# Batch 0's attention in f32 straight from the inputs, its probabilities turned by TensorE, its chunks in the order 1, 0, 2

## The chip, the cores and the metric

The kernel runs on one core of one Trainium2 chip. Its metric is the device time in microseconds (us), here the median of three executions. A measurement of it tells a difference of about 1% from none. PE is TensorE, PEld its weight loads, DVE VectorE, ACT ScalarE, POOL GpSimd, SP SyncE; POOL and SP here mostly copy and issue transfers, and ACT's queue issues the loads of the inputs.

## The reference, cut to what matters

Block-sparse attention over four batches, eight heads, 768 positions of 64 numbers, and a bilinear FFN (512 to 1536 to 512) on its result. A query block of 32 rows sees its own block and its neighbours, the first and the last block, and three drawn blocks; the first and the last query block see everything.

```python
scores = scale * np.matmul(q, k.transpose(0, 1, 3, 2))
mask = np.abs(blk_i - blk_j) <= window
mask = mask | (blk_i == 0) | (blk_j == 0) | (blk_i == n_blocks - 1) | (blk_j == n_blocks - 1)
for qb in range(n_blocks):
    for kb in sampled_blocks[qb]:
        mask[qb * block:(qb + 1) * block, kb * block:(kb + 1) * block] = True
scores = np.where(mask, scores, -1000000000.0)
scores = scores - np.max(scores, axis=-1, keepdims=True)
attn = np.exp(scores)
attn = attn / (np.sum(attn, axis=-1, keepdims=True) + 1e-09)
x = np.matmul(attn, v)          # then (3072, 512)
a = x @ w_a
b = x @ w_b
return (a * b @ w_out).astype(np.float32)
```

q, k, v and the drawn blocks are f32 and int64, the three weights float64.

## The kernel before

**Units and chunks.** A unit is one query block of one batch with all eight heads (24 units a batch; units 0 and 23 are dense, the others sparse with 256 keys). Eight units are a chunk of 256 tokens, three chunks a batch, twelve in all. Every operand of a matmul that isn't f32r is split into a high and a low f16 part, and a product is three products (high by high, high by low, low by high).

**Preparation.** `keys` loads one pair of heads of K, finds its largest value (ACT, L477), a scale of a power of two (`set_scale`: POOL, then three DVE steps), and makes both parts (ACT L482, DVE L483); SP turns them by a DMA transpose into `keysT`. `values` does the same for V (L522, L523) and stores the parts in DRAM (`vd`). `queries` does it for a chunk (L637 to L644) and copies the parts to the other half of the partitions over SP. `weights` turns float64 bits into f32 (three DVE steps, L699, L702, L705) and splits: the columns of w_a and w_b into f16 parts (`wab`, ACT L719 and L726, DVE L727), w_out into two f32r parts (`woh`, `wol`, L732 and L733). The staging space of the weights is that of K and V of later batches and of `keysT[1]`, so batch 1 starts its loads behind the last weight (`w_freed`).

**Attention.** For a sparse unit POOL copies the keys that it sees into `KG`, SP fetches its values into `VG`; `attend` sends a mask product (L853) and 16 score products (L752) to PE, the largest score (DVE L868), the exponentials with sums (ACT L878), the reciprocal, and `in_parts` splits the probabilities (ACT L770 or DVE L773, then DVE L777) into `hl`. SP turns `hl` by a DMA transpose into `pt`; 24 value products (L796) follow. A dense unit goes the same way in four pieces (`attend_quad`, `all_values`). Each pair of units gives `xT` (ACT L1040, DVE L1043).

**FFN.** `first_products` sends 24 products (L1078) a column f of 128, twelve columns a chunk, into one of two PSUM banks `ab`; `inner` multiplies both halves, `split` makes the f32r parts, `second_products` sends six products (L1166 to L1168) a column into `o`. The second chunk in order is parked: its products are stored in DRAM and fetched back later (`parked_g`).

**What sets the order.** The kernel is written as flows (generators) that yield steps; a planner gives each engine's steps a place by the costs, ranks and events written beside them, and the program is that list. Each engine then runs its list in order, waiting where a semaphore says so. `units` and its numbers `order` set which unit comes when; rings (`take`) bound how many buffers are in use.

Of the kernel before, what the change touches and what calls it, by code (L numbers as in the profile page):

```python
# [18 lines left out]
NB = 24  # L19
# [223 lines left out]
def kernel(  # L243
# [9 lines left out]
    c_blocks: bass.AP,  # L253
    out: bass.AP,
# [51 lines left out]


# [18 lines left out]

    k_ready = [Event(NG) for _ in range(B)]
# [5 lines left out]
    q_ready = [Event(3) for _ in range(NC)]  # L333
    tables = Event()
    mask_ready = Event()
    units = [(b, i) for b in range(B) for i in range(NB)]
# [42 lines left out]
    def make_tables():  # L379
# [3 lines left out]
        row = work.tile([P, DM], F32, tag="st", name="mrow", bufs=ST_BUFS)  # L383
        held2 = yield from take("st", ST_BUFS)
# [9 lines left out]
        def load():  # L394
# [7 lines left out]
            nc.scalar.dma_start(cb, c_blocks)  # L402

        yield [Way("ACT", 300, load, 250)]
# [43 lines left out]
    def raw_tile(b, g, n):  # L448

        if b == 0:  # L450
            late = wab[:, NF // 2 :].rearrange("p f i a c x -> p (f i a c x)").bitcast(F32)
            late = late.rearrange("p (g x) -> p g x", x=2 * NT * D)
            return late[:, n * NG + g], parked
# [8 lines left out]
    parked = Event(2 * NG)  # L462

    def keys(b, g):
        yield from gate(order[b, 0] - GATE_KV)
# [4 lines left out]
        elif b > 0:  # L470
# [27 lines left out]
    def values(b, g):  # L498
# [17 lines left out]
        if g == NG - 1:  # L516
            plan.start(values_scale(b), order[b, 0] - LEAD_V)
        yield v_scale[b]
# [33 lines left out]

    def gather_keys(n):
# [8 lines left out]
        to = KG[n % KG_BUFS].bitcast(I32)  # L562
        of = keysT[b % 2].bitcast(I32)
        w = BLK // 2
        first = i <= KG_BUFS

        def copies():
# [4 lines left out]
            for r, at in enumerate(dynamic("POOL", offs_k, i)):  # L572
# [7 lines left out]

    def gather_values(n):
# [3 lines left out]
        yield v_stored[b]  # L585
# [3 lines left out]
        to = VG[n % VG_BUFS]  # L589
        first = i <= VG_BUFS  # L590

        def copies():
            if i in (0, NB - 1):
                hq, x1 = divmod(x, 2)
                nc.sync.dma_start(
                    to.rearrange("p a x -> p (a x)")[:, : 3 * ROW // HQ].rearrange(
                        "p (t x) -> p t x", t=3
                    ),
                    vd[b][x1 * HALF : (x1 + 1) * HALF, hq * ROW // HQ : (hq + 1) * ROW // HQ]
# [3 lines left out]
            nc.sync.dma_start(to[0 : 3 * BLK, 0, :], vd[b][(i - 1) * BLK : (i + 2) * BLK, :])  # L603
            if first:
                nc.sync.dma_start(to[3 * BLK : P, 0, :], vd[b][0:BLK, :])
                nc.sync.dma_start(to[0:BLK, 1, :], vd[b][(NB - 1) * BLK :, :])
            for r, at in enumerate(dynamic("SP", offs, i)):
                nc.sync.dma_start(  # L608
                    to[(1 + r) * BLK : (2 + r) * BLK, 1, :], vd[b][bass.ds(at, BLK), :]
                )  # L610

        dense = i in (0, NB - 1)
# [660 lines left out]
```

## Time and profile before

| | |
|---|---|
| median of three executions | 959.56 us (955.2 to 962.41) |
| span of the profiled execution, first to last instruction | 943.8 us (23,877 instructions) |
| its own time | not listed apart from the three; span and median differ by 15.8 us |
| PE busy | 784.2 us, 83% |
| DVE busy | 580.2 us, 61% |
| ACT busy | 459.2 us, 49% |
| POOL busy | 173.6 us, 18% |
| DMA | 145.24 MB, 154 GB/s on average |

Busy time is the union of an engine's instructions; matmuls are pipelined, so a group's mean duration is longer than the distance from one start to the next, and prices of matmuls are read from starts. Idle time of an engine that nobody waits for costs nothing.

### The profile page before, as it was taken

Reading aid. Unit: us, or ns where it says so; the run is one execution under the profiler, and the core shown is the slowest. Engines: PE = TensorE matmul, PEld = TensorE weight load, DVE = VectorE, ACT = ScalarE, POOL = GpSimd, SP = SyncE. Lnnn points to the kernel's source line nnn. Section 1 sums busy time; section 2 is a strip of 40 time slices with the busy share of each in tenths; the row PEclk is TensorE's granted clock in tenths of the full one; section 3 lists DMA queues with packets and bytes.
Section 4 is the critical chain, followed back from the end, with each engine's and each line's share of the span. In section 5 each row is a group of like instructions: output and inputs, shape, how many; then the busy total and the mean of one; then the engine's idle time right before and its main releaser. Section 6 shows DMA issues by size and latency. Waiting matters only on the chain.

```text
span 943.8 us, 23877 instructions
## 1 busy us (share of the span) xinstructions
PE 784.2 (83%) x9024; PEld 628.9 (67%) x9024; DVE 580.2 (61%) x1593; ACT 459.2 (49%) x1097; POOL 173.6 (18%) x416
## 2 busy tenths in 40 slices
PE   0133388868978889989989989999999999999998
PEld 0022267646756767778767877777777778888886
DVE  3797899985646766755667766555764735432222
ACT  4665455685525655744455566334554424332222
POOL 0344320221003433100233221000441300000000
PEclk9999589988998999999999999999999999999999
DMA  9999998489878779894775995644675605432000
GB/s 260 252 237 181 217 246 239 130 218 167 202 183 175 157 160 233 193 193 110 161 166 130 249 164 141 155 99 124 163 152 122 139 1 138 111 79 63 22 2 23
DMA packets 212030, 145.24 MB, mean 154 GB/s; under 512 B 152777, under 2 KB 180426, under 8 KB 211146
## 3 DMA queue, kind: packets, MB, share of 16 engines
q1 hardware_dynamic: 201088, 105.95, 52.0%
q10 hardware_dynamic: 10826, 37.76, 13.9%
q8 instruction: 71, 1.16, 0.5%
q14 instruction: 45, 0.37, 0.1%
HBM read 87.56 MB, written 14.16 MB: 108 GB/s over the span
## 4 chain that ended last, share of the span: by engine, by line
PE 42%; DMA 24%; DVE 18%; ACT 7%; SPq 5%; issue 4%; ACTq 0%; POOL 0%; DVEq 0%
PE ab L1078 23%; DMA pt<-hl 12%; PE o L1166 4%; PE av L796 4%; PE o L1168 4%; PE o L1167 4%; DVE hl L777 3%; PE s L752 2%; DMA VG<-vd 2%; DVE hl L773 2%; DMA q<-in_q_dram 2%; ACT sm L878 2%; DVE low L868 2%; SPq L608 1%; DVE xT L1043 1%
## 5 line engine op out<-in xcount | busy, mean ns | idle before, releaser
L1078 PE MATMUL ab<-xT,wab 128*128 128x256 f16 x3456 | 410.8, 277 | 12.8 <-ACT xT L1040 5.0
L1078 PEld LDWEIGHTS <-wab 128*128 128x128 f16 x3456 | 332.4, 99 | 85.1 <-issue 38.0
L1113 DVE TENSOR_TENSOR a<-a,ab 128x256 f32<-128x256 f32 x144 | 60.2, 418 | 122.5 <-ACT a L1110 121.1
L878 ACT ACTIVATE sm<-s,low,cq 128x256 f32<-128x256 f32 x176 | 98.1, 560 | 76.4 <-DVE hl L777 44.1
L1166 PE MATMUL o<-woh,gh 128*128 128x512 f32 x288 | 126.9, 441 | 8.1 <-ACT gh L1135 7.9
L1110 ACT ACTIVATE a<-ab,f 128x256 f32<-128x256 f32 x144 | 67.7, 470 | 134.1 <-PE ab L1078 126.7
L796 PE MATMUL av<-pt,VG 128*128 128x64 f16 x2688 | 107.4, 198 | 27.3 <-DMA VG<-vd 17.7
L796 PEld LDWEIGHTS <-VG 128*128 128x128 f16 x2688 | 98.3, 101 | 46.9 <-issue 36.4
L777 DVE SCALAR_TENSOR_TENSOR hl<-sm,den,hl 128x256 f16<-128x256 f32 (+1 forms) x208 | 106.1, 516 | 16.4 <-ACT hl L770 14.3
L1168 PE MATMUL o<-woh,gl 128*128 128x512 f32 x288 | 115.3, 400 | 1.0 <-DVE gl L1138 1.0
L1167 PE MATMUL o<-wol,gh 128*128 128x512 f32 x288 | 113.8, 395 | 0.0
L568 POOL COPY KG<-keysT 128x384 int32<-128x384 int32 x88 | 52.5, 596 | 318.6 <-PE s L752 285.2
L573 POOL COPY KG<-keysT 128x128 int32 x264 | 95.3, 398 | 42.4 <-POOL KG L568 30.7
L773 DVE TENSOR_SCALAR hl<-sm,den 128x256 f16<-128x256 f32 (+1 forms) x140 | 53.3, 382 | 60.8 <-DMA pt<-hl 60.5
L1135 ACT CAST gh<-a 128x256 fp32r<-128x256 f32 x132 | 53.2, 403 | 68.9 <-DVE a L1113 68.0
L752 PEld LDWEIGHTS <-QT 128*32 128x32 f16 x1664 | 45.3, 104 | 50.8 <-issue 46.5
L853 PE MATMUL s<-mrows,ident 128*32 128x192 bf16 (+1 forms) x352 | 26.2, 286 | 63.2 <-ACT sm L878 41.3
L1138 DVE TENSOR_TENSOR gl<-a,gh 128x256 fp32r<-128x256 f32 x132 | 58.2, 441 | 32.6 <-ACT gh L1135 31.1
L1166 PEld LDWEIGHTS o<-woh,gh 128*128 128x128 f32 x288 | 54.6, 190 | 28.0 <-ACT gh L1135 11.5
L1043 DVE SCALAR_TENSOR_TENSOR xT<-av,xT 64x256 f16<-64x256 f32 x96 | 40.4, 421 | 52.2 <-ACT xT L1040 51.1
L1168 PEld LDWEIGHTS o<-woh,gl 128*128 128x128 f32 x288 | 54.7, 190 | 16.2 <-DVE gl L1138 3.8
L853 PEld LDWEIGHTS <-ident 128*32 128x32 bf16 x352 | 11.9, 94 | 76.7 <-issue 67.8
(93 smaller groups left out, 797.9 us busy)
## 6 DMA issues: line engine op xcount, KB each, us to landing
VG<-vd SPq DMA_DIRECT2D x280, 64.0 KB, 2.5
VG<-vd SPq DMA_DIRECT2D x88, 192.0 KB, 3.5
VG<-vd SPq DMA_DIRECT2D x32, 384.0 KB, 3.6
q<-in_q_dram ACTq DMA_DIRECT2D x12, 512.0 KB, 5.7
QT<-QT SPq DMA_DIRECT2D x24, 256.0 KB, 4.2
vd<-vs SPq DMA_DIRECT2D x16, 384.0 KB, 3.9
out_dram<-ou SPq DMA_DIRECT2D x24, 256.0 KB, 3.3
stage<-in_k_dram ACTq DMA_DIRECT2D x12, 384.0 KB, 5.7
```

Source lines behind the costliest of these rows:

```text
L573: nc.gpsimd.tensor_copy(to[:, :, (5 + r) * w : (6 + r) * w], of[:, :, bass.ds(at, w)])
L752: mm(to[h * BLK : (h + 1) * BLK], q_block(cc, i, 4 * hq + h, a), rhs(4 * hq + h), start=(first and a == 0), stop=(a == 1), skip_group_chec ...
L773: Way("DVE", 227 + n * 0.49, lambda: nc.vector.tensor_scalar(hi, sm, over, None, ALU.mult), 0, X_HIGH),
L777: t = yield dve(221 + n * 1.03, lambda: nc.vector.scalar_tensor_tensor(lo, sm, over, hi, ALU.mult, ALU.subtract))
L796: mm(av[:, g, i % 2, :], w, pt[:, y, cols], start=(i % 2 == 0 and g == 0 and first and n + m == 0), stop=(last and n == len(terms) - 1 and ...
L878: t = yield act(750, lambda hq=hq: nc.scalar.activation(sm[:, hq], ps[:, hq], AF.Exp, bias=low[:, at, hq, 0:1], scale=cq[:, cc, hq : hq + ...
L1078: mm(ab[:, i, :], wab[:, f, i, part, kt, :], xc[:, kt, a, :], start=(i == 0 and kt == 0 and part + a == 0), stop=(kt == KT - 1 and a == 1) ...
L1110: yield act(470, lambda: nc.scalar.activation(a_sb, ab[:, 0, :], AF.Copy, scale=fb[:, f : f + 1]))
L1113: t = yield dve(420, lambda: nc.vector.tensor_mul(a_sb, a_sb, ab[:, 1, :]))
L1166: mm(po, gh[:, js], woh[:, f, :], start=(f == 0), stop=False)
L1167: mm(po, gh[:, js], wol[:, f, :], start=False, stop=False)
L1168: mm(po, gl[:, js], woh[:, f, :], start=False, stop=(f == NF - 1))
```

## The change

For batch 0 alone, nothing is split. K is laid out on the host as it is used (head pair on the partitions, keys along) and loaded into `keysT[0]` as f32; V is laid out by position and gathered from the input itself, so `vd` of batch 0 isn't written; only V's largest value is still taken, for the scale of x, which moves into `output_half`. Queries are loaded into a tile of which one half of the partitions is zero (even heads have the upper half zero, odd heads the lower), so that one product over 128 rows takes one head of a pair. Scores are 8 f32 products a sparse unit instead of 16, values 8 instead of 24. The probabilities are normalised in place (`plain_norm`), turned by four f32 transposes on PE into a PSUM bank of the ring `ab` (`plain_turn`, against an identity that is loaded as a new constant), and copied to `pt`. The bank of `ab` is the one that the FFN's products use.

The order of batch 0's chunks is 1, 0, 2 (`seq`): the eight sparse units 8 to 15 come first, then dense unit 0 with 1 to 7. The first chunk in order is not parked, the second is, as before. The queries' rows of all batches are laid out even heads first.

```diff
+    plain_keys = keysT[0].rearrange("p h s -> p (h s)").bitcast(F32).rearrange(
+        "p (g s) -> p g s", g=NG
+    )
+    plain_values = v[0].rearrange("g p x -> (g p x)").rearrange("(s x) -> s x", x=H * D)
...
+    seq = [1, 0, *range(2, NC)]
+    place = {cc: p for p, cc in enumerate(seq)}
...
-    units = [(b, i) for b in range(B) for i in range(NB)]
+    units = [divmod(cc, NCH) for cc in seq]
+    units = [(b, c * PER + x) for b, c in units for x in range(PER)]
...
     def keys(b, g):
+        if b == 0:
+            t = yield load_way(1000, lambda: nc.scalar.dma_start(plain_keys[:, g], k[0, g]))
+            k_ready[0].fire(t)
+            if g + 1 < NG:
+                plan.start(keys(0, g + 1), -LEAD_K)
+            return
...
         v_bound[b].fire(end)
         if g == NG - 1:
             plan.start(values_scale(b), order[b, 0] - LEAD_V)
+        if b == 0:
+            freed.fire(end)
+            return
...
+    def plain_queries(cc, u0):
+        q_used[cc] = yield from take("QT", QT_BUFS)
+        t = work.tile([P, 2, NG, CH], F32, tag="QT", name=f"QZ{cc}", bufs=QT_BUFS)
+        QT[cc] = t
+        parts_of = [slice(0, D), slice(D, P)]
+        def blank():
+            for y in range(2):
+                nc.gpsimd.memset(t[parts_of[1 - y], y], 0.0)
+        end = yield pool(1800, blank)
+        for y in range(2):
+            end = yield load_way(700, lambda y=y: nc.scalar.dma_start(
+                t[parts_of[y], y], q[0, cc, :, y * NG : (y + 1) * NG]
+            ))
+            q_ready[cc].fire(end)
+        next_queries(cc)
...
+    def plain_scores(to, cc, i, hq, rhs, first):
+        r = i % PER * BLK
+        for h in range(4):
+            g, y = divmod(4 * hq + h, 2)
+            mm(
+                to[h * BLK : (h + 1) * BLK], QT[cc][:, y, g, r : r + BLK], rhs(g),
+                start=first, stop=True, skip_group_check=True,
+            )
...
+    def plain_norm(sm, over, n):
+        return [
+            Way("DVE", 150 + n * 0.53, lambda: nc.vector.tensor_scalar(
+                sm, sm, over, None, ALU.mult
+            )),
+            Way("ACT", 290 + n * 0.83, lambda: nc.scalar.activation(
+                sm, sm, AF.Copy, scale=over
+            )),
+        ]
+    def plain_turn(sm, pt, name, freed):
+        cols = pt.shape[1]
+        yield eye_ready
+        read = yield from take("ab", 2)
+        ps = psum.tile([P, cols, P], F32, tag="ab", name=f"tp{name}", bufs=2)
+        def turns_():
+            for x in range(cols):
+                nc.tensor.transpose(ps[:, x], sm[:, x * P : (x + 1) * P], eye[0])
+        t = yield pe(110 * cols, turns_)
+        freed.fire(t)
+        eye_used.fire(t)
+        n = cols * P
+        t = yield [
+            Way("ACT", 220 + n * 0.83, lambda: nc.scalar.copy(pt, ps)),
+            Way("DVE", 160 + n * 1.04, lambda: nc.vector.tensor_copy(pt, ps)),
+        ]
+        read.fire(t)
+        return t
...
+        if b == 0:
+            yield dve(165, lambda: nc.vector.tensor_scalar(dn, dn, EPS, None, ALU.add))
+            yield dve(160, lambda: nc.vector.reciprocal(dn, dn))
...
+            for hq in range(HQ):
+                yield plain_norm(sm[:, hq], den[:, at, hq, 0:1], NK)
...
+            yield from plain_turn(sm.rearrange("p a k -> p (a k)"), pt, f"{n}", freed)
...
-        if cc >= 2:
-            yield ffn_done[cc - 2]
+        p = place[cc]
+        if p >= 2:
+            yield ffn_done[seq[p - 2]]
+        if b == 0:
+            yield v_scale[0]
...
+        s = float(2.0 ** -14)
+        if cc < NCH:
+            s = scale[half * 64 : half * 64 + 64, at_v : at_v + 1]
```

Where the lists of the engines change, at three places (names with a number are buffers). SP's queue near its start, before: `keysT` is K turned, `QT` the queries' second half, `vd` V's parts in DRAM.

```order
L491 DMA_TRANSPOSE keysT_77<-ks_3_144 128x12x128
L668 DMA QT_140<-QT_140 64x2048
L527 DMA vd_79<-vs_2_306 128x6x256
L527 DMA vd_79<-vs_3_307 128x6x256
L527 DMA vd_79<-vs_1_308 128x6x256
L995 DMA_TRANSPOSE pt_00_350<-hl_00_334 128x6x128
L527 DMA vd_79<-vs_0_340 128x6x256
```

SP's queue at its start now: the gathers of the first two units' values, from the input.

```order
L647 DMA VG_85<-in_v_dram 96x512
L649 DMA VG_85<-in_v_dram 32x512
L650 DMA VG_85<-in_v_dram 32x512
L573 TENSOR_LOAD offs
L652 ISA
L652 DMA VG_85<-in_v_dram 32x512
```

Ahead of the first sparse unit's gather (L603) stood 21 transfers of the preparation and of the first dense unit; now none does.

DVE's list up to the last x step of the first chunk (`xT`), before: splitting probabilities (`hl`) and weights (`wol`, `wab`) stand side by side.

```order
L733 TENSOR_TENSOR wol<-w_1007,woh 128x512
L375 RECIPROCAL scale<-rscale 128x2
L702 SCALAR_TENSOR_TENSOR wab<-stage,wab 128x512
L777 SCALAR_TENSOR_TENSOR hl_1281<-sm_1175,den,hl_1281 128x256
L705 SCALAR_TENSOR_TENSOR wab<-stage,wab 128x512
L727 SCALAR_TENSOR_TENSOR wab<-wab,scale 128x512 x2
L699 TENSOR_SCALAR wab<-stage 128x512
L1043 SCALAR_TENSOR_TENSOR xT_87<-av_6_1277,xT_87 64x4x64 x2
```

The same place now (`pt` is the copy of turned probabilities, `tp` the PSUM bank); it is row 133 of the list instead of 248.

```order
L801 TENSOR_TENSOR wol<-w_389,woh 128x512
L386 RECIPROCAL scale<-rscale 128x2
L773 SCALAR_TENSOR_TENSOR wab<-keysT_78,wab 128x512
L770 SCALAR_TENSOR_TENSOR wab<-keysT_78,wab 128x512
L795 SCALAR_TENSOR_TENSOR wab<-wab,scale 128x512
L948 COPY pt_00_785<-tp_00_786 128x384
L795 SCALAR_TENSOR_TENSOR wab<-wab,scale 128x512
L1211 SCALAR_TENSOR_TENSOR xT_87<-av_14_735,scale,xT_87 64x4x64 x2
```

The same x step comes after fewer weight steps, and no split of probabilities stands ahead of it.

PE's list ahead of the first product of the FFN (`ab`), before: the value products of the first chunk's last units end in it.

```order
L853 LDWEIGHTS ident
...
L752 LDWEIGHTS QT_140
...
L796 LDWEIGHTS VG_85
L796 MATMUL av_6_1277<-pt_1173,VG_85 128x64
L1078 LDWEIGHTS wab
L1078 MATMUL ab_0_1431<-xT_87,wab 128x256
```

The same place now (`s_00` to `s_11` are scores of dense unit 0):

```order
L878 MATMUL av_12_611<-pt_638,VG_86 128x64 x8
L878 MATMUL av_14_735<-pt_680,VG_85 128x64 x8
L820 MATMUL s_10_757<-keysT_77,QZ_130 32x384 x4
L940 MATMUL tp_00_786<-eye,sm_00_753 128x128 x3
L878 MATMUL av_14_735<-pt_716,VG_86 128x64 x8
L820 MATMUL s_11_763<-keysT_77,QZ_130 32x384 x4
L940 MATMUL tp_01_818<-eye,sm_01_756 128x128 x3
L1246 LDWEIGHTS wab
L1246 MATMUL ab_0_826<-xT_87,wab 128x256
```

The first product stands behind the first half of the dense unit, its scores and its turns.

## Rows read from the trace of the kernel before

**Rows 1.** The page, slices: TensorE, busy tenths in 40 equal slices.

```profile
PE   0133388868978889989989989999999999999998
```

**Rows 2.** Windows of the span: busy time of each engine, granted clock, DMA share.

```profile
core 0: us, PE busy (x) PEld busy (x) DVE busy (x) ACT busy (x) POOL busy (x), PEclk, DMA share, GB/s
0.00:125.40 125.40, 32.65 (x532) 23.65 (x533) 94.17 (x255) 71.47 (x152) 40.30 (x82) 0.89 0.99 231
125.40:189.00 63.60, 56.08 (x572) 45.17 (x571) 60.36 (x161) 37.73 (x89) 11.34 (x22) 0.92 0.72 199
189.00:272.00 83.00, 66.65 (x678) 51.58 (x676) 51.78 (x145) 47.59 (x109) 11.02 (x31) 0.92 0.85 191
272.00:431.00 159.00, 138.76 (x1815) 109.89 (x1813) 107.62 (x307) 89.54 (x217) 40.81 (x100) 0.96 0.86 184
431.00:944.00 513.00, 490.02 (x5436) 398.57 (x5432) 266.27 (x729) 212.89 (x533) 70.09 (x181) 1.00 0.49 114
```

**Rows 3.** Timeline of PE around the first product: start, us, engine, line, what, idle before.

```profile
125.44 0.58 PE L1078 MATMUL ab<-xT,wab 128*128 128x256 f16 x2 [3.65 <-ACT xT L1040]
...
132.68 0.86 PE L796 MATMUL av<-pt,VG 128*128 128x64 f16 x24
...
133.47 0.27 PE L853 MATMUL s<-mrows,ident 128*32 128x192 bf16 x4
...
133.56 0.61 PE L752 MATMUL s<-KG,QT 128*32 128x256 f16 x16
...
134.10 2.79 PE L1078 MATMUL ab<-xT,wab 128*128 128x256 f16 x24
...
136.74 0.86 PE L796 MATMUL av<-pt,VG 128*128 128x64 f16 x24
...
137.75 0.39 PE L1167 MATMUL o<-wol,gh 128*128 128x512 f32 x1
...
137.98 0.40 PE L1168 MATMUL o<-woh,gl 128*128 128x512 f32 x1
```

**Rows 4.** Timeline of DVE: the last weight's step L733, same columns.

```profile
188.67 0.69 DVE L733 TENSOR_TENSOR wol<-w,woh 128x512 fp32r<-128x512 f32 x1
```

**Rows 5.** Groups by line, DVE: count, busy us, mean ns, idle before.

```profile
L777 DVE SCALAR_TENSOR_TENSOR hl<-sm,den,hl 128x256 f16<-128x256 f32 (+1 forms) x208 | 106.1, 516 | 16.4 <-ACT hl L770 14.3
...
L773 DVE TENSOR_SCALAR hl<-sm,den 128x256 f16<-128x256 f32 (+1 forms) x140 | 53.3, 382 | 60.8 <-DMA pt<-hl 60.5
...
L644 DVE SCALAR_TENSOR_TENSOR QT<-q,scale,QT 64x2048 f16<-64x2048 f32 x12 | 28.2, 2349 | 8.7 <-ACT QT L642 8.7
...
L727 DVE SCALAR_TENSOR_TENSOR wab<-wab,scale 128x512 f16<-128x512 f32 x16 | 12.1, 768 | 0.0
...
L483 DVE SCALAR_TENSOR_TENSOR ks<-stage,scale,ks 128x768 f16<-128x768 f32 x12 | 11.9, 1014 | 1.1 <-ACT ks L482 1.0
...
L1182 DVE COPY ou<-o 128x512 f32<-128x512 f32 x13 | 8.8, 687 | 1.8 <-PE o L1168 1.8
...
L733 DVE TENSOR_TENSOR wol<-w,woh 128x512 fp32r<-128x512 f32 x12 | 8.4, 701 | 0.0
...
L705 DVE SCALAR_TENSOR_TENSOR w<-keysT,w 128x512 int32<-128x512 int32 x10 | 7.0, 704 | 0.0
...
L702 DVE SCALAR_TENSOR_TENSOR w<-stage,w 128x512 int32<-128x512 int32 x10 | 6.8, 682 | 0.0
...
L699 DVE TENSOR_SCALAR w<-keysT 128x512 int32<-128x512 int32 x10 | 4.2, 428 | 0.0
```

**Rows 6.** Groups by line, PE and its weight loads (PEld), same columns.

```profile
L1078 PE MATMUL ab<-xT,wab 128*128 128x256 f16 x3456 | 410.8, 277 | 12.8 <-ACT xT L1040 5.0 <-ACT wab L726 4.1 <-DVE power L369 2.1
...
L796 PE MATMUL av<-pt,VG 128*128 128x64 f16 x2688 | 107.4, 198 | 27.3 <-DMA VG<-vd 17.7 <-DMA pt<-hl 6.5 <-DVE xT L1043 2.8
...
L796 PEld LDWEIGHTS <-VG 128*128 128x128 f16 x2688 | 98.3, 101 | 46.9 <-issue 36.4 <-DMA VG<-vd 8.4 <-DMA keysT<-in_moe_w_out_dram 0.4
...
L1168 PEld LDWEIGHTS o<-woh,gl 128*128 128x128 f32 x288 | 54.7, 190 | 16.2 <-DVE gl L1138 3.8
```

More of the change, by code (lines that the diff above doesn't have):

```diff
@@ L383, in make_tables @@
         row = work.tile([P, DM], F32, tag="st", name="mrow", bufs=ST_BUFS)
+        rings.setdefault("hl", Ring(HL_BUFS)).freed.append(eye_used)
+        whole = work.tile([P, 2 * HQ * NK // 2], F32, tag="hl", name="eye", bufs=HL_BUFS)
+        eye[0] = whole[:, :P]
         held2 = yield from take("st", ST_BUFS)
@@ L452, in raw_tile @@
             late = late.rearrange("p (g x) -> p g x", x=2 * NT * D)
[L453 removed]
+            return late[:, g], parked
         yield w_freed
@@ L879, in attend @@
                 sm[:, hq], ps[:, hq], AF.Exp, bias=low[:, at, hq, 0:1],
-                scale=cq[:, cc, hq : hq + 1], accum_out=den[:, at, hq, 0:1],
+                scale=factor_of(b, cc, hq), accum_out=den[:, at, hq, 0:1],
             ))
         read.fire(t)
+        if b == 0:
+            yield dve(165, lambda: nc.vector.tensor_scalar(dn, dn, EPS, None, ALU.add))
+            yield dve(160, lambda: nc.vector.reciprocal(dn, dn))
+            mine = yield from turn("hl", b, i)
+            mine.fire(0)
+            for hq in range(HQ):
+                yield plain_norm(sm[:, hq], den[:, at, hq, 0:1], NK)
+            mine = yield from turn("pt", b, i)
+            kept = yield from take("pt", PT_BUFS)
+            mine.fire(0)
+            pt = work.tile([P, 2 * HQ, P], F32, tag="pt", name=f"pt{n}", bufs=PT_BUFS)
+            yield from plain_turn(sm.rearrange("p a k -> p (a k)"), pt, f"{n}", freed)
+            yield vg_ready[b, i, 0]
+            yield from before(b, i)
+            vg = plain_vg(m)
+            quads = [
+                (hq, [
+                    (pt, 2 * hq + x, None, vg[:, x, hq * 4 * D : (hq + 1) * 4 * D])
+                    for x in range(2)
+                ])
+                for hq in range(HQ)
+            ]
+            t = yield from values_into(b, i, quads, True, True)
+            kept.fire(t)
+            vg_free[m].fire(t)
+            return
         yield dve(165, lambda: nc.vector.tensor_scalar(
@@ L983, in attend_quad @@
         mine_pt = yield from turn("pt", b, i, hq)
+        if b == 0:
+            mine.fire(0)
         for x in range(2):
+            if b == 0:
+                yield plain_norm(sms[x], d1, HALF)
+                kept = yield from take("pt", PT_BUFS)
+                if x == 1:
+                    mine_pt.fire(0)
+                pt = work.tile([P, 3, P], F32, tag="pt", name=f"pt{n}_{hq}{x}", bufs=PT_BUFS)
+                t = yield from plain_turn(sms[x], pt, f"{n}_{hq}{x}", freed[x])
+                plan.start(all_values(b, i, hq, x, pt, kept), n, t)
+                continue
             gone = yield from take("hl", HL_BUFS)
@@ L1146, in second_products @@
         banks, o_read = [None] * NJ, [None] * NJ
-        for cc in range(NC):
+        for cc in seq:
             b, c = divmod(cc, NCH)
-            if cc == 1 and PARK:
+            if place[cc] == 1 and PARK:
                 plan.start(unpark(), R_NOW)
@@ L1193 @@
         plan.start(keys(0, 0), -LEAD_K)
-        plan.start(queries(0), -LEAD_Q)
+        plan.start(queries(seq[0]), -LEAD_Q)
         plan.start(make_tables(), 0)
```

192 lines of the change are left out of this document (119 added, 73 removed).

## The prediction

> **What bounds the kernel now.** I read the slices of the page first [rows 1]: TensorE (PE) is nearly idle in the first eighth of the span and full in the second half. The windows [rows 2] put times to it and show the other engines. Up to 125.4 us PE is busy for 32.7 us only, DVE for 94.2, DMA all the time. From 431 us to the end PE is busy for 490 of 513 us: that part is PE's and can shrink only if its work shrinks. In between, 125.4 to 431 us, PE has 261.5 of 305.6 us. So there are 137 us of idle PE ahead of 431 us, and a change of the start is worth what it takes out of them.
>
> Two dates matter. The first product of the FFN stands at 125.44 us; its releaser is an x step, ACT's L1040 [rows 3]: it waits for the eight units of the first chunk. The last weight is split at 188.7 us (L733, [rows 4]); products of the last column f = 11 and batch 1's loads, which reuse the staging space, wait for that. Up to this date DVE has 154.5 busy us of 189, so DVE's list of work paces it.
>
> **What the change does to the last date.** I counted DVE's instructions in the order of each kernel up to the twelfth `wol` and priced them by [rows 5]. Before: 142 weight steps (36 L699 at 0.42, 36 L702 at 0.68, 36 L705 at 0.70, 22 L727 at 0.76, 12 L733 at 0.70: 90 us), 8 splits of K and V at 1.01 (8.1), 3 of queries at 2.35 (7.0), 34 low parts of probabilities at 0.52 and 14 high parts at 0.38 (22.9), and 54 us of reductions, x steps and small ones: 182 us in all, of which the trace shows 154.5 busy, since neighbours overlap (factor 0.85). After: the same 142 weight steps; the 15.1 us of splits and the 22.9 us of parts are gone; new are 24 normalisations (f32 from f32, 128x256; no such row, so between nothing and the 0.38 of L773; I take 0.3: 7.2 us) and 9 copies of turned probabilities out of PSUM (128x512 f32, the shape of L1182: 0.69, 6.2 us); seven triples of scale steps and six factors less give back 4.7, a few more small steps cost 1.5. Together 27.8 us less, times 0.85: **-23.6 us**, if the 34.5 idle us of DVE stay. The last weight is then split at 165 us.
>
> Is DMA late next? By 189 us it has moved about 42 MB (the GB/s of [rows 2]). The change drops four turns of keys, four stores of values, four copies of queries and all turns of batch 0's probabilities; the loads are the same bytes apart from a 64 KB identity. What must land by the last weight is K and V (3.1 MB), 18.9 MB of weights, queries (1.0) and values for 17 units (0.38 MB each, 1.5 for the dense one: 7.7): 31 MB, at 231 GB/s 134 us. It hides under DVE. Of the queues, SP now holds only gathers there, whose transfers are as large as before, and ACT loses its passes over K, V and queries; POOL copies the same number of 4-byte words, and its clearing of the query tile lies in the first 10 us, in which it waits. These cost nothing, and nothing leaves the path with them.
>
> **The first date.** Up to the x step that opens the first product DVE's list is 111 us before and 53 after (41 weight steps stand ahead of it, not 76, and the dense unit 0 stands behind): 94.2 busy us become 45. With the same 31 idle us the first product comes at 76 us, 49 earlier. This isn't gained as such: the first pass over the columns needs all twelve weights, so it ends no earlier than 165 us. What it gives is room to do PE's work in.
>
> **PE's work.** Prices at full rate from [rows 3], start to start: a group of 24 products 2.64 us, 16 scores of 256 columns 0.54 (four heads side by side in the array, 34 ns each), 4 mask products 0.09, 24 value products 0.79 (33 ns each), a product of 512 columns with a 4-byte operand 0.23. A sparse unit costs 1.42 us. No row shows a plain f32 product. The cheapest it can be is one pass like L1166 to L1168; for the other end I use what the kernel itself does: a 4-byte number is two halves, a full product of two of them four half products. I take four, because three are what this kernel needs for less precision. Then scores are 8x4x0.034 = 1.08, values 8x4x0.033 = 1.05, mask 0.09. A turn of 128x128 lies between 128 columns of such a row (0.06) and a bare load of its 4-byte weights, 0.19 [rows 6]; I take 0.12, four of them 0.5. The unit is 2.72 us, **1.3 more** (with one pass throughout 0.85, 0.6 less). [...]
>
> [...]
>
> Up to the first product PE idles for 92.7 of 125.4 us, so the first eight units' extra is hidden. From 76 to 165 us PE has, by the order, 15 groups of products (four of them of the chunk that is parked, moved up as filler), 11 groups of second products at 1.4 and nine more units at 2.7, with the dense one some 82 us in 89. Before it had 56.1 in 63.6 there (88%); at that rate 82 us take 93: **+4 us** on the date. Behind it, up to 431 us, the order of before has 35 groups of products, 34 of second products and 9 units of batch 0 left; that of after 31, 33 and 7. That is -4x2.64 - 1.4 - 2x1.42 + 7x1.3 = **-5.7 us**. From the first dense unit of batch 2 on, the two orders of PE are the same to the end (10,265 rows), and so are those of the other engines from about there; I count nothing behind 431 us.
>
> **The wait that is added.** Before, a unit's probabilities were turned by DMA while PE went on; PE stood for 27.3 us ahead of its value products over the 96 units [rows 6], 0.28 each. Now PE's own queue holds the turn: it waits for the normalisation, and the products and scores queued behind it wait as well; then the value product waits for the copy. I charge one such wait more per unit, 24x0.28 = **+7 us** (0 if the planned distance holds).
>
> Sum: -23.6 + 4 - 5.7 + 7 = -18.3. The profiled span is 943.8 us; its run's own time isn't listed apart, and the median of three is 959.56, 15.8 above the span, which stays. So **941 us**.
>
> **Rivals.** (a) *PE's f32 is dearer, and the kernel slower.* If four heads in f32 don't run side by side, a score product costs the 0.11 of a whole-array one (2.64/24): 8x4x0.11 = 3.5 us per unit instead of 1.08, over the 16 units behind the first product 39 us: 980. It turns slower than before once a unit costs 18.3/16 = 1.15 us more than my 2.72. For it: loads of 4-byte weights take 0.19 against 0.10 for 2-byte ones [rows 6]. Against it: before 125 us there is room for half of the units.
> [...]
> (b) *The turns block the FFN.* They use the two PSUM banks `ab` of the products. If each of the 20 turns behind the first product keeps a bank for its copy (0.69 and a hop of 0.2) while a group of products waits, 18 us go: 959, no change. For it: PE is full there. Against it: the banks wait little now (L1078 stands idle for 12.8 us in 3,456 products).
> (c) *More comes off.* If the waits and the lateness are nothing (-11) and f32 products need one pass (another 13 for seven units), it is 917. For it: 16.4 idle us of PE between 189 and 272, part of them behind DMA turns that are gone.
>
> **How the numbers follow.** The forecast has 0.42, (a) 0.16, (b) 0.22, (c) 0.20. About 1% (9.6 us) is what a measurement of this kernel can tell from no change. Faster by more: 0.42 + 0.20 = 0.62; within: 0.22; slower: 0.16. The range goes down to (c) with its margin, 915, and up past (b) to 965; outside are (a) and a little of (c).
>
> **What would show it.** Right: the first product near 76 us, the last `wol` near 165, about 17 units turned by then, PE rows for f32 scores near 1.1 us per unit, and the first dense scores of batch 2 near 413 us instead of 431. Wrong: a last weight later than 175 us with DVE full (my list lacks something), or with DVE idle (DMA or a ring paces it); PE full from 76 to 165 us but behind (f32 price); idle PE ahead of turns of over 0.5 us each (the added wait).

## The result, and the profile after

The changed kernel takes 928.5 us (median of 4 runs, 923.0 to 932.8) against 961.0 us for the kernel before on the same chip (4 runs, 955.2 to 969.2): a ratio of 0.971, with a 95% interval from 0.964 to 0.978. On a second chip, with more runs, it was 926.8 against 949.0, 0.977 (0.973 to 0.981). So it is faster by 2 to 3%, where 1.9% was forecast (941 of 959.56); the measured time lies inside the forecast's range, 12.5 us below the 941 us. A ratio leaves out executions more than 1.5% above the fastest of the same kernel; medians and ranges of times count all.

The profiled execution of the changed kernel spans 928.7 us, against 943.8 us. The page of the changed kernel, its first line of busy times and TensorE's slices, answers to [rows 1]:

```profile
PE 835.5 (90%) x8912; PEld 669.1 (72%) x8912; DVE 549.9 (59%) x1527; ACT 435.8 (47%) x1074; POOL 169.3 (18%) x415
...
PE   0788987899998787989999999999989999999998
```

PE was busy for 784.2 of 943.8 us before. Now it is busy for 51.3 us more and idle for 93.2 us in place of 159.6, which is 66.4 us less; the span is their difference, 15.1 us shorter. The second slice has gone from 1 to 7: apart from the first slice, the idle eighth at the start is mostly filled.

The windows of the changed kernel, the columns of [rows 2]:

```profile
0.00:125.40 125.40, 87.33 (x752) 67.00 (x756) 86.27 (x245) 59.64 (x153) 37.68 (x82) 0.86 0.66 205
125.40:189.00 63.60, 51.50 (x401) 39.55 (x394) 56.61 (x149) 37.32 (x86) 15.05 (x29) 0.89 0.49 154
189.00:272.00 83.00, 81.44 (x780) 65.49 (x778) 50.58 (x139) 45.21 (x109) 15.55 (x39) 1.00 0.73 175
272.00:431.00 159.00, 139.05 (x1664) 109.01 (x1664) 99.00 (x285) 84.10 (x204) 32.05 (x84) 0.97 0.76 163
```

Up to 125.4 us PE does 87.3 us of work in place of 32.7, and DMA's share falls from 0.99 to 0.66. From 189 to 272 us PE is full (81.4 of 83, from 66.7), and the granted clock there is 1.00 in place of 0.92.

The dates, from timelines of PE and DVE in the changed kernel (the first product, the last weight's step, the first dense scores of batch 2; the first two answer to [rows 3, 4]):

```profile
81.90 3.11 PE L1246 MATMUL ab<-xT,wab 128*128 128x256 f16 x23
...
178.93 0.68 DVE L801 TENSOR_TENSOR wol<-w,woh 128x512 fp32r<-128x512 f32 x1
...
413.25 0.83 PE L829 MATMUL s<-keysT,QT 128*32 128x384 f16 x16
```

The first product comes at 81.9 us (125.4 before, 76 forecast). The last weight is split at 178.9 us (188.7 before, 165 forecast). The first dense scores of batch 2 stand at 413.25 us, where 413 was forecast (430.2 before), and from there to the end it is 515.5 us (513.6 before): the whole gain lies ahead of this date.

The groups of the changed kernel, which answer to [rows 5, 6] and show the new kinds (the recorder lists two matmuls for each f32 product):

```profile
L1246 PE MATMUL ab<-xT,wab 128*128 128x256 f16 x3456 | 407.3, 275 | 3.6 <-DVE a L1281 2.8 <-DVE wab L795 0.5
L878 PE MATMUL av<-pt,VG 128*128 128x64 f16 (+1 forms) x2464 | 138.0, 212 | 22.1 <-DMA VG<-vd 15.6 <-DVE xT L1211 2.8 <-DVE pt L948 1.4
...
L820 PE MATMUL s<-KG,QZ 128*32 128x256 f32 x352 | 28.2, 450 | 0.0
...
L940 PE MATMUL tp<-eye,sm 128*128 128x128 f32 x112 | 21.8, 325 | 7.5 <-DVE sm L924 4.5 <-ACT sm L927 2.6 <-DVE pt L948 0.4
...
L878 PEld LDWEIGHTS av<-pt,VG 128*128 128x128 f32 x448 | 59.9, 213 | 7.5 <-DVE pt L948 2.9 <-issue 1.8 <-ACT pt L947 1.8
...
L924 DVE TENSOR_SCALAR sm<-sm,den 128x256 f32<-128x256 f32 (+1 forms) x41 | 14.4, 360 | 0.3
```

The FFN's products (L1246) stand idle for 3.6 us in all, less than the 12.8 of [rows 6]. The turns (L940) wait for 7.5 us.

A sparse unit's new price stands in PE's timeline of the changed kernel, around one unit and around one group of value products with work right behind it:

```profile
162.66 1.89 PE L878 MATMUL av<-pt,VG 128*128 128x64 f32 x16
164.39 1.80 PE L1246 MATMUL ab<-xT,wab 128*128 128x256 f16 x15
...
167.01 0.60 PE L940 MATMUL tp<-eye,sm 128*128 128x128 f32 x4
167.54 0.27 PE L971 MATMUL s<-mrows,ident 128*32 128x192 bf16 x4
167.63 1.04 PE L820 MATMUL s<-KG,QZ 128*32 128x256 f32 x16
168.60 2.00 PE L878 MATMUL av<-pt,VG 128*128 128x64 f32 x16
```

Start to start: four turns 0.53, the mask 0.09, eight scores 0.97, eight value products 1.73 (162.66 to 164.39). That is 3.3 us, against 1.42 before and 2.72 forecast; all of the miss is in the value products (1.05 forecast).

Where the idle time went is in the view of PE's waits (who waited, for whom, us in total, times, longest). First before, up to 430 us:

```profile
PE s L752 <- DMA QT<-QT: 37.3, 1, 37.3
PE s L853 <- ACT sm L878: 35.8, 15, 10.0
PE s L853 <- ACT sm L970: 14.0, 3, 8.0
...
PE s L853 <- DVE power L369: 6.4, 1, 6.4
PE av L796 <- DMA pt<-hl: 6.3, 2, 4.5
PE s L752 <- ACT sm L970: 6.1, 4, 2.5
```

And of the changed kernel, up to 413 us:

```profile
PE s L971 <- DVE mrows L453: 21.5, 1, 21.5
PE s L971 <- ACT sm L999: 15.4, 9, 4.5
...
PE av L878 <- DMA VG<-vd: 10.2, 8, 3.3
```

Two waits make up most of it. The first scores waited 37.3 us for the split queries' turn; now the first wait is 21.5 us. Scores that waited for ACT's exponentials, which free the two banks of `s`, cost 55.9 us (35.8, 14.0 and 6.1); now 16.8 (15.4, and 1.2 and 0.2 in rows not shown). Together that is 55 of the 66 us. Neither is the last weight, on which the prediction built its sum. A shorter wait in such a list isn't a gain by itself, as the run of the chunk order alone shows below.

### The profile page after: what moved, and what is told of

It reads as the page before. It is cut to its first block, busy times and chain, and to the rows that moved or that the text cites. A ratio compares the mean times of both kernels' runs of the same rounds, so it can differ in the third digit from the quotient of the medians.

```text
span 928.7 us, 23488 instructions
## 1 busy us (share of the span) xinstructions
PE 835.5 (90%) x8912; PEld 669.1 (72%) x8912; DVE 549.9 (59%) x1527; ACT 435.8 (47%) x1074; POOL 169.3 (18%) x415
## 4 chain that ended last, share of the span: by engine, by line
PE 52%; DMA 18%; DVE 15%; ACT 6%; SPq 5%; issue 3%; ACTq 0%; POOL 0%; POOLq 0%; DVEq 0%
PE ab L1246 24%; DMA pt<-hl 10%; PE av L878 8%; PE o L1334 5%; PE o L1336 4%; PE o L1335 4%; DMA keysT<-ks 2%; DVE hl L854 2%; PE s L820 2%; ACT sm L999 2%; DVE xT L1211 2%; SPq L652 2%; PE tp L940 2%; DVE hl L850 2%; ACT xT L1210 1%
## 5 line engine op out<-in xcount | busy, mean ns | idle before, releaser
L1246 PE MATMUL ab<-xT,wab 128*128 128x256 f16 x3456 | 407.3, 275 | 3.6 <-DVE a L1281 2.8
L1246 PEld LDWEIGHTS <-wab 128*128 128x128 f16 x3456 | 330.9, 99 | 73.6 <-issue 34.0
L878 PE MATMUL av<-pt,VG 128*128 128x64 f16 (+1 forms) x2464 | 138.0, 212 | 22.1 <-DMA VG<-vd 15.6
L603 POOL COPY KG<-keysT 128x384 int32<-128x384 int32 (+1 forms) x88 | 52.0, 591 | 347.2 <-PE s L829 240.3
L999 ACT ACTIVATE sm<-s,low,cq 128x256 f32<-128x256 f32 x132 | 73.6, 561 | 65.0 <-DVE hl L854 33.1
L608 POOL COPY KG<-keysT 128x128 int32 (+1 forms) x264 | 91.8, 385 | 40.7 <-POOL KG L603 26.0
L878 PEld LDWEIGHTS <-VG 128*128 128x128 f16 x2016 | 69.3, 98 | 34.7 <-issue 23.5
L850 DVE TENSOR_SCALAR hl<-sm,den 128x256 f16<-128x256 f32 (+1 forms) x117 | 43.6, 374 | 66.4 <-DMA pt<-hl 66.3
L854 DVE SCALAR_TENSOR_TENSOR hl<-sm,den,hl 128x256 f16<-128x256 f32 (+1 forms) x156 | 78.8, 513 | 6.2 <-ACT hl L847 4.6
L1336 PEld LDWEIGHTS o<-woh,gl 128*128 128x128 f32 x288 | 54.3, 188 | 17.3 <-DVE gl L1306 5.0
L878 PEld LDWEIGHTS av<-pt,VG 128*128 128x128 f32 x448 | 59.9, 213 | 7.5 <-DVE pt L948 2.9
L986 DVE TENSOR_REDUCE low<-s 128x2 f32<-128x512 f32 x88 | 59.9, 681 | 7.6 <-PE s L820 5.6
L1335 PEld LDWEIGHTS o<-wol,gh 128*128 128x128 f32 x288 | 54.8, 190 | 6.7
```

The costliest lines, as they stand in the source:

```text
L608: nc.gpsimd.tensor_copy(to[:, :, (5 + r) * w : (6 + r) * w], of[:, :, bass.ds(at, w)])
L850: Way("DVE", 227 + n * 0.49, lambda: nc.vector.tensor_scalar(hi, sm, over, None, ALU.mult), 0, X_HIGH),
L854: t = yield dve(221 + n * 1.03, lambda: nc.vector.scalar_tensor_tensor(lo, sm, over, hi, ALU.mult, ALU.subtract))
L878: mm(av[:, g, i % 2, :], w, pt[:, y, cols], start=(i % 2 == 0 and g == 0 and first and n == 0), stop=(last and n == len(each) - 1), skip_g ...
L986: yield dve(685, lambda: nc.vector.tensor_reduce(mx, ps, axis=mybir.AxisListType.X, op=ALU.max, negate=True))
L999: t = yield act(750, lambda hq=hq: nc.scalar.activation(sm[:, hq], ps[:, hq], AF.Exp, bias=low[:, at, hq, 0:1], scale=factor_of(b, cc, hq) ...
```

## The experiments

Theory D is the prediction's: DVE's list up to the last weight paces the start. Theory E came out of the waits above: what counts is that the attention starts early and that PE stands idle less often behind ACT.

### The kernel before, again

Nothing is edited.

> The kernel before, unchanged. Theory A (time is span plus a fixed small amount, and the profiled execution shown of before was a quick one): a span some 2 us under its own time, so 953 to 965 us, and the extra 10 to 20 us over the first profile lies ahead of 431 us, in waits for DMA. Theory B (some 16 us lie outside the span): a span near 944 again beside a time near 960.

It took 943.9 us (10 runs, 939.1 to 954.7) beside 946.6 for its twin: 0.9987 (0.9947 to 1.0028). Its profiled run spans 946.3 us and took 948.1, so 1.8 us lie around the span. Theory A's fixed small amount holds, its 953 to 965 us doesn't. The 15.8 us of the prediction were thus not a constant: the profiled execution of before was a quick one (943.8 + 1.8 = 945.6), and the three runs shown with it were not. Chips and executions differ by 1 to 2% (medians of the kernel before lie between 943.9 and 961.0 us, its 10 runs here between 939.1 and 954.7), so everything below goes by ratios. The forecasts of the runs are in us beside some 960 us for the kernel before, so they are read as ratios too.

### The chunk order taken back, and the chunk order alone

```diff
-    seq = [1, 0, *range(2, NC)]
+    seq = list(range(NC))
```

> The changed kernel with batch 0's chunks in the order 0, 1, 2, so the dense unit stands first again. Theory A (the date of the last weight and PE's fill decide, the first product's date is only room): first product some 10 us later than 82 us, last weight within 5 us of 179, time within 1% of the changed kernel's 928. Rival (the early first product is the gain): about 10 us slower than the changed kernel, 938 or more.

922.5 us, ratio 0.977 (0.970 to 0.984): as fast as the change. Its first product comes at 90.7 us and its last weight at 173.1, near Theory A's dates. The other way round, the order second, first, third in a kernel without the rest of the change:

> The kernel before with nothing but the order of batch 0's chunks changed to 1, 0, 2: everything is split and turned by DMA as before. Theory C: no change beyond 1% (0.99 to 1.01 of before), the first product some 10 us earlier than 125 us, since the dense unit's four pieces go behind it. Rival (the order is the change's gain): 0.98 or less.

949.1 us, 1.0015 (0.998 to 1.005). The order is worth nothing measurable, with or without the rest. Its trace also tells what a wait's name is worth. PE's waits up to 428 us, among them:

```profile
PE s L967 <- DVE mrows L449: 33.3, 1, 33.3
PE av L874 <- DMA VG<-vd: 28.6, 12, 4.7
PE s L967 <- ACT sm L995: 23.0, 11, 4.0
...
PE s L825 <- POOL KG L604: 11.9, 2, 10.4
```

With the order alone, the scores' waits for ACT are already 32.6 us (23.0, and 4.7, 3.2 and 1.7 in rows not shown) in place of 55.9, yet PE's idle time is 160.6 us against 159.6: waits for the values `VG` (28.6 in place of 8.5) and the keys `KG` stand there instead.

### Keys and queries as loaded, alone

Values are split and the probabilities are cut and turned by DMA as before; of batch 0 only the scores are f32.

```diff
 def values / gather_values / attend / attend_quad / output
-        if b == 0:
+        if False:
...
-        each = 240 if b == 0 else 180
+        each = 180
```

> One part alone: scores in f32 from K and queries as loaded, chunks 1, 0, 2; V, probabilities (two parts, turned by DMA) and value products as in the kernel before. Theory A (each part gives what it takes off DVE and PE): DVE loses 11 us of splits ahead of the first product, PE keeps the cheap value products: first product near 100 us, last weight near 183, time 940 to 948. Rival (the early start alone is the gain): 930 or less. Rival (turns by DMA held the kernel): 955 or more.

924.5 us, 0.982 (0.974 to 0.990); span 919.4 us, PE busy for 799.5. The first product comes at 88.8 us and the last weight at 176.3. In us this is the first rival's 930 or less; beside 960 us, Theory A's 940 to 948 is 0.979 to 0.988 and that rival's 930 is 0.969, so by ratio the size is A's. Its dates came 11 and 7 us earlier than A has them.

### Values as loaded and turns on TensorE, alone

The other half: keys and queries are split as before.

```diff
 def keys / gather_keys / queries
-        if b == 0:
+        if False:
...
-        heads = plain_scores if b == 0 else scores
+        heads = scores
```

> The other part alone: V as loaded, probabilities in f32 turned by PE, value products in f32, chunks 1, 0, 2; K and queries split and scores in f16 as before. Theory A: first product near 105 us, last weight near 180, time 940 to 948. Rival (the DMA turns and the stores of V were what held the kernel): 930 or less. Rival (f32 value products and turns are a loss by themselves): 958 or more.

943.4 us, 0.997 (0.993 to 1.001): no change. Beside 960 us Theory A's 940 to 948 is 0.979 to 0.988, so by ratio A is out; the first product came at 101.2 us, the last weight at 201.4, 21 us later than A has it. PE's budgets of five profiled executions, each worked out from the span and PE's busy time on the page, show why:

| kernel | span | PE busy | PE idle |
|---|---|---|---|
| before | 943.8 | 784.2 | 159.6 |
| order alone | 944.1 | 783.5 | 160.6 |
| keys and queries | 919.4 | 799.5 | 119.9 |
| values and turns | 938.8 | 829.6 | 109.2 |
| all (the change) | 928.7 | 835.5 | 93.2 |

Values and turns take 50.4 us of idle time away and put 45.4 us of work in its place. Keys and queries take 39.7 us away for 15.3 of work. Both halves draw on the same idle time: together they remove 66.4 us, not 90, and still pay 51.3 us of work, of 60.7 for the two. These are single profiled executions. The measured times don't tell halves that add from halves that don't: the halves' 1.8% and 0.3% make 2.1%, and the whole gives 2.3% (1.9 to 2.7).

### The changed kernel, and keys and queries in the order first, second, third, with more runs

> The changed kernel, unchanged, to stand beside the others on one chip. If the two kernels keep their ratio: 0.971 of before. If the traces give the difference (913 to 929 us is what two profiles of before, 943.8 and 946.3 us, and one of after, 928.7, leave): 0.98 of before.

926.8 us, 0.977 (0.973 to 0.981); this is the second chip of the result. The interval takes in 0.98 and leaves out 0.971. The profiled execution has its last weight at 183.7 us, 4.8 later than the first one of this kernel.

> K and queries as loaded alone, as in the earlier run, but with batch 0's chunks in the order 0, 1, 2. Theory C (the gain is the K and query part; the order is worth nothing): within 1% of the same part with order 1, 0, 2, 0.98 of before. Rival (the sparse chunk first is what that part needs, since V's parts and stores stand ahead of the dense unit's values): 10 us slower than it.

924.0 us, 0.975 (0.971 to 0.979), on the same chip, as Theory C has it; the rival's 10 us are out. The two intervals overlap: within what they tell, half of the change does all that the whole does, and no version tried that computes the whole result is shown to beat it.

### Half of the f32 value products left out

This kernel leaves out 104 of batch 0's 224 value products, and with them part of its attention's sums.

```diff
+            if b == 0 and len(each) > 1:
+                each = each[: (len(each) + 1) // 2]
```

> The changed kernel with 104 of the 224 f32 value products of batch 0 left out (of two products on a sum one, of three two), so part of the attention's sums is missing; order and all else are the same. A product takes 0.22 us on PE in the trace after, so 23 us of PE's work are gone, two thirds of it behind the first product. Theory A (PE's f32 work is on the path up to the last weight): 10 to 15 us faster than the changed kernel. Rival (it is hidden by DVE's list): within 4 us of it.

916.3 us, 0.958 (0.951 to 0.965), beside 0.977 for the changed kernel in the same comparison: by the ratios 18.7 us less (11 to 26), by the medians 10.5. At 1.73/8 = 0.22 us a product, 23 us of PE's work went: by the ratios half to all of it comes off the time. That is Theory A's 10 to 15 us or more, and the rival's 4 us are out: PE's f32 work in the start isn't hidden.

### The planner told the true price of the value products

```diff
-        each = 240 if b == 0 else 180
+        each = 430 if b == 0 else 180
```

> The changed kernel with one number of its planner altered: batch 0's f32 value products are priced at 430 ns a pair in place of 240, near what the trace shows; only the order of instructions changes, nothing is left out. Theory (their cost is work that TensorE must do, and the order hides what can be hidden): within 5 us of the changed kernel's 927, 922 to 930. Rival (the low price makes the order wrong, so TensorE waits): 8 us or more off, 919 or less.

935.0 us, 0.982 (0.976 to 0.987), beside 0.977 of the changed kernel on another chip: the intervals overlap, and the gain of 8 us that the rival expected (0.969) lies outside. In us the theory's 922 to 930 is missed; by ratio the kernel is some 4 us above the changed one, within its 5. The low price isn't what keeps the values from paying. The last weight came at 172.5 us here, 6.4 us earlier than in the changed kernel's first trace, and the time isn't shorter.

### Keys loaded later

The kernel with keys and queries as loaded (0.975) and one wait more.

```diff
 def keys(b, g):
         if b == 0:
+            yield w_bound[0]
```

> The kernel with keys and queries as loaded in the order 0, 1, 2 (924 us), with one line more: batch 0's key loads wait for the bound of the first weight column. Nothing is left out; the attention starts some 12 to 15 us later. Theory E (the gain of plain keys and queries is that the first scores stand at 15 to 22 us instead of 37): the most of the gain goes, 934 to 939 us, the last weight at about 188. Theory D (VectorE's list up to the last weight paces, the early start is by the way): VectorE does weight steps in the time that is freed, 929 us or less, the last weight no more than 5 us later than 176.

933.9 us, 0.983 (0.978 to 0.987): 0.7% slower than 0.975, with an interval of 0.1 to 1.3% (some 7 us, 1 to 13). This and the next two runs come from another chip than the 0.975, each set beside its own runs of the kernel before; 0.982 and 0.975 for keys and queries alone, in two orders, are as far apart. Its first scores, from the timeline of PE:

```profile
23.96 1.60 PE L817 MATMUL s<-keysT,QZ 128*32 128x384 f32 x4 [23.96 <-DMA keysT<-in_k_dram]
```

And its last weight's step, from the view of the tile `wol` on DVE (duration in ns, min, median and max, then first and last start in us):

```profile
L798 DVE TENSOR_TENSOR wol<-w,woh x1: 673/673/673, 162.0 to 162.0; 128x512 fp32r<-128x512 f32 x1
```

The attention starts 9 us later (23.96 us against 14.90), not the 12 to 15 that I had counted on, and the last weight is split 14 us *earlier* (162.0 against 176.1). If that date set the end, the kernel would be faster. It is slower by an amount between the two forecasts; the sign is E's. E's mechanism isn't seen, though. PE's line of the page without the added wait (span 920.4 us) and with it (927.2 us):

```profile
PE 794.3 (86%) x9024; PEld 624.8 (68%) x9024; DVE 564.9 (61%) x1556; ACT 435.9 (47%) x1079; POOL 174.9 (19%) x415
...
PE 805.4 (87%) x9024; PEld 630.9 (68%) x9024; DVE 561.3 (61%) x1548; ACT 442.5 (48%) x1087; POOL 173.0 (19%) x415
```

PE is idle for 126.1 us without it and 121.8 with it: the late start left no more idle time. What grew is the busy time of the same 9,024 matmuls, by 11.1 us, with a mean granted clock of 0.954 in place of 0.967. So this run doesn't show that the early start is the gain.

### VectorE given the work back

```diff
+            plan.start(fill(g, P, 2 * NT * D, 1070), -LEAD_K, t)
...
+        plan.start(fill(NG + cc, D, H * CH, 2350), u0 - LEAD_Q, end)
...
+        yield pool(900, lambda: nc.gpsimd.memset(t[:parts, :size], 0.0))
+        end = yield dve(ns, lambda: nc.vector.scalar_tensor_tensor(
+            t[:parts, :size], t[:parts, :size], 0.5, t[:parts, :size], ALU.mult, ALU.subtract
+        ))
```

> The kernel with keys and queries as loaded in the order 0, 1, 2 (924 us), with about as much dummy work put back on VectorE as the splits of keys and queries took there: four steps of 128x768 at 1.0 us and three of 64x2048 at 2.35 us, on scratch. Nothing is left out. Theory D (VectorE's list paces up to the last weight): 11 us times the 0.85 of the prediction, of which the four early steps fall in its first idle time: some 6 us slower, 930. Theory E (the early start is the gain, VectorE has room): within 3 us of 924.

939.8 us, 0.985 (0.979 to 0.990): 0.9% slower, with an interval of 0.2 to 1.6% (some 9 us, 2 to 15). That is nearer to D's 6 us than to E's 3 at most, but the interval begins at 2. Each dummy also puts a clearing of its scratch on POOL, priced at 0.9 us, seven in all, which stand in the queue of the key copies. So the run points to VectorE's work in the start without showing it, and by which wait the dummies reach the end stays open.

### The weights' low parts on GpSimd

Theory D would have the twelve subtractions moved off VectorE:

```diff
-            end = yield dve(680, lambda: nc.vector.tensor_sub(lo, w, hi.bitcast(F32)))
+            end = yield pool(1300, lambda: nc.gpsimd.tensor_sub(lo, w, hi.bitcast(F32)))
```

> The kernel with keys and queries as loaded in the order 0, 1, 2 (924 us), with the twelve low parts of the output weights subtracted on GpSimd in place of VectorE. Nothing is left out. Theory D: 12 x 0.7 x 0.85 = 7 us off VectorE's list, the last weight at about 169 and the time 917. Rival (GpSimd's step is slower and stands ahead of its key copies, or TensorE is full by then): no gain, 922 to 930, though VectorE has more idle time.

1010.1 us, 1.062 (1.057 to 1.067): far outside both forecasts. POOL's timeline of this kernel (start, us, what, idle before):

```profile
113.35 1.25 POOL L797 TENSOR_TENSOR wol<-w,woh 128x512 fp32r<-128x512 f32 x1 [7.45 <-PE av L874]
121.05 0.37 POOL L377 PARTITION_ALL_REDUCE power<-bound  x1 [6.45 <-issue]
121.31 0.57 POOL L599 COPY KG<-keysT 128x384 f32<-128x384 f32 x1
121.76 1.29 POOL L604 COPY KG<-keysT 128x128 f32 x3
130.59 1.35 POOL L797 TENSOR_TENSOR wol<-w,woh 128x512 fp32r<-128x512 f32 x1 [7.54 <-ACT sm L995]
131.90 0.55 POOL L599 COPY KG<-keysT 128x384 f32<-128x384 f32 x1
```

The step itself takes 1.25 us, as priced. But between 60 and 200 us, ahead of every subtraction that follows a reduction over partitions (L377), and of every such reduction that follows a subtraction, POOL stands for 6 to 8 us; ahead of the reductions all of it is put down to nothing that the profile shows ("issue"). Copies behind either have no gap. In the kernel without the move, POOL's timeline has this reduction straight behind a key copy:

```profile
93.88 0.52 POOL L377 PARTITION_ALL_REDUCE power<-bound  x1
```

The views of the two lines have a record of POOL's sequencer (POOLq), MODIFY_POOL_CONFIG (first this kernel, L377 and L797; last L377 of the kernel without the move):

```profile
L377 POOLq MODIFY_POOL_CONFIG  x26: 1/7/10, 2.7 to 265.6; - x26
L797 POOLq MODIFY_POOL_CONFIG  x24: 3/45/85, 37.0 to 253.9; - x24
...
L377 POOLq MODIFY_POOL_CONFIG  x2: 4/4/4, 2.7 to 2.7; - x2
```

That is 50 records in place of 2: by their number, two at each of the 24 changes from one kind to the other. Behind the subtraction at 96.43 us, for instance, which takes 1.25 us, POOL stands for 6.03 us until the reduction at 103.71. The two kinds alternate once per column, so each column costs some 14 us of POOL's queue (7.45 and 6.45 in the rows above), and the last weight comes at 264 us. What POOL does in the gaps isn't shown; the rows show the gaps, and these records at both lines. PE's scores then wait 67.2 us for ACT (L995; 31.3 without the move) and 17.3 us for POOL's key copies, so the late weight isn't the only thing that the gaps delay.

## Why the prediction was right, and where it wasn't

**The sum.** Forecast was -18.3 us; the profiled spans differ by -15.1, the medians on the second chip by -22 and on the first by -32.5. By ratio 0.981 was forecast and 0.971 and 0.977 were measured: the direction was right, the size somewhat low. The 941 us came out 12.5 too high largely because of the step "15.8 above the span, which stays": 1.8 us stay, and on 945.6 us the sum gives 927.3, against 928.5 measured (the kernel before took 946.6, 949.0 and 952.3 us in the later comparisons). That the sum comes so near is in good part luck: its terms were off in both directions, and the path that its largest term stands on isn't what gave the gain.

**The last date.** "The last weight is then split at 165 us" failed; it was 178.9. The list itself was near: DVE has 134 busy us up to there, where 154.5 - 23.6 = 131 were forecast. What failed was "if the 34.5 idle us of DVE stay": they grew to 45. A last weight later than 175 us with DVE idle is one of the signs of being wrong that the prediction itself named. DVE's waits up to 179 us in the changed kernel begin with

```profile
DVE mrow L423 <- DMA mrow<-in_sampled_blocks_dram: 14.6, 1, 14.6
DVE xT L1211 <- ACT xT L1210: 11.9, 6, 2.2
```

where the same two were 4.7 and 4.0 us before: DVE has less work in its first microseconds (4.2 busy us of the first 24, 9.0 before), so part of what was taken off its list became a wait at its head. More important, the date isn't what the time hangs on. Among the kernels that gain, it moved between 162 and 184 us without the time following: 162.0 with 0.983, 172.5 with 0.982, 173.1 with 0.977, 176.1 with 0.975, 176.3 with 0.982, and 178.9 and 183.7 with the change itself. The kernels that gain nothing do have later dates (188.7 before, 191.9 with the order alone, 201.4 with values and turns), but there too the latest isn't the slowest. At 264 us the time rose by 6%, with POOL's other work late as well.

**PE's work.** The unit's 2.72 us were 3.3. Scores (1.08 forecast, 0.97), turns (0.5, 0.53) and mask were right; four half products was the right count for scores. "Values 8x4x0.033 = 1.05" failed: 1.73. The 33 ns are a product of 2-byte weights, whose loads overlap (0.098 us each, one every 0.033 us); the f32 form loads its 128x128 weights twice per product, 0.192 us each (median), and its matmuls stand 0.108 us apart. Over the 16 units behind the first product the 0.68 us that were missing make 11 us of PE's work. Of the 23 us left out in the run above, 18.7 (11 to 26) came off the time, so the term was mis-sized by some 9 us of time (estimate, 11 x 18.7/23). Between the two dates the forecast of PE's lateness was met: 85.2 busy us in 97.0 (88%), where 82 in 93 were forecast.

**The added wait.** +7 was charged. The turns and the value products behind their copies stand idle for 9.4 us (7.5 of L940; 1.4 and 0.5 of L878 behind `pt`), and the waits for DMA's turns that they replaced, 6.3 us up to 430, are gone: some +3 net. The turns stand for 0.25 us a group (7.5 over 30), below the 0.5 that the prediction named as a sign of being wrong.

**The clock** has no term in the sum. From 189 to 272 us the granted clock went from 0.92 to 1.00, with PE busy for 81 of 83 us in place of 67; at the level of before, PE would have done some 0.08 x 83 = 6.6 us less there (estimate). No run set the clock apart from PE's work, though the late keys show busy time alone growing by 11.1 us (1.4%) at a granted clock of 0.954 in place of 0.967.

**The dates near the end.** 413 us for the first dense scores of batch 2 was met to a fraction of a us, though the terms before it were off in both directions: DVE's idle time and the values' price against a first wait that is 16 us shorter and scores that wait 39 us less behind ACT. The prediction had these gains within "137 us of idle PE", but counted on DVE's list for them.

**The rivals.** (a) is refuted: sixteen f32 matmuls, in four column groups, start within 0.97 us, 0.06 apart, where one lasts 0.38. (b) is refuted: the FFN's products wait 3.6 us in place of 12.8, and where it counted a hop of 0.2 us, ACT's copy starts 0.09 us behind a group of turns (67.24 to 67.33 us). (c) needed f32 in one pass, 0.27 us for eight scores (8x0.034), which the rows exclude with 0.97; its time (917) is reached only with value products left out.

**What carries the gain.** Shown by the two halves: keys and queries as loaded are worth the whole of it, within what the comparisons tell; values as loaded with turns on TensorE are worth nothing measurable, alone or, in either chunk order, on top of the other half. Which effect of keys and queries as loaded carries the gain stays open. Three go together: the first scores stand at 15 to 22 us in place of 37, DVE is busy for 566.5 us in place of 580.2, and ACT for 435.1 in place of 459.2 (order second, first, third). The late keys and the dummy work cost 7 and 9 us (each give or take 6, and measured on another chip), and neither changed one thing alone. ACT's relief, for which PE's longest waits before speak, wasn't tried by itself. The other half takes as much off DVE (565.2) and nothing off ACT (461.2) and gains nothing, but it also pays 45.4 us of PE's work, so it doesn't decide.

## What to carry to other kernels

Where one engine is full to the end, make the sum in its idle time ahead of that point: list its waits, price what each edit takes out of them and what work it puts in, and remember that two edits that draw on the same idle time needn't add. A date that looks like a gate is worth moving only if the full engine waits for it by name in that list, and even then another wait can take its place, as the order alone did here. When a variant is slower, look first whether the full engine's idle time grew or its busy time. And split a change along its operands before keeping all of it: here half of it gives the whole gain.

## What the runs showed of the hardware

- An f32 product is two matmuls in the trace, and each of 256 columns takes 379 ns (median) where the 2-byte form takes 273. The difference, 106 ns, is near the 110 ns from start to start of the FFN's 2-byte products of 256 columns (2.64/24 us, [rows 3]); by that, a record holds two passes and a product four (estimate, worked out from these durations alone). Four column groups in f32 still run side by side: 16 such matmuls start 0.061 us apart.
- For few columns f32 costs more than its passes: value products of 64 columns cost 0.108 us per matmul with its load, against 0.033 in 2-byte form, though by the point above the stream of one should be 128 columns, 0.053 us (half of the 106 ns; estimate). What the rest is wasn't tried; the loads, which last 0.192 us (median) in place of 0.098, may be it.
- Four f32 turns of 128x128 in a row cost 0.53 us start to start, 0.13 each, though each lasts 273 ns (median).
- With the weights' low parts on GpSimd, POOL stands for 6 to 8 us (60 to 200 us into the span) each time it goes between a subtraction of two tensors and a reduction over partitions, with two records MODIFY_POOL_CONFIG a change by their number (50 in place of 2), and a copy behind either starts with no gap.
